# Two quarters of the combined weights made in one stay of small tiles

## The chip, the core and the metric

The kernel runs on one core of a Trainium2 chip. It is written in a language in which every instruction is given to an engine by the program: TensorE (PE in the profile) multiplies matrices, VectorE (DVE), ScalarE (ACT) and GpSimd (POOL) do the element work, SyncE (SP) issues the transfers. The engines run side by side, each takes its own instructions in order, and semaphores hold an instruction until its inputs are there and its buffer is free. The metric is the time of one execution on the device in microseconds (us); lower is better.

## The reference

Eight batches of attention with eight heads, 576 positions and 64 columns a head. Keys and values are first gathered by 32 packed queries of each head, then the full queries attend to the packed values; the result goes through a gated layer of 2048 columns, on 8 x 576 = 4608 rows.

```python
def sm_attn(qq, kk, vv):          # scale = 1/sqrt(64)
    s = scale * qq @ kk.T
    a = exp(s - max(s)); a = a / (sum(a) + 1e-09)
    return a @ vv
p_packed = sm_attn(p, k, v)              # (8, 8, 32, 64)
out = sm_attn(q, p_packed, p_packed)     # (8, 8, 576, 64)
x = out, heads side by side              # (4608, 512)
h = x @ w_in                             # w_in (512, 2048)
g = h * clip(h + 3, 0, 6) / 6
result = g @ w_out                       # w_out (2048, 512), all float32
```

## The kernel before

The second attention ends in a product with the packed values, and the layer begins with a product with w_in. Both are linear, so the kernel multiplies the packed values of a batch with w_in once: the **combined weights** M. The first product of the layer is then the attention weights a times M. M of a batch is made in four **quarters**, of 512 columns of w_in each; a quarter is two banks of PSUM. Each factor of a large product is split into a high and a low part (a_hi and a_lo, m_hi and m_lo), and three products of parts stand for one.

TensorE can be used as one tile of 128 x 128 or as several small tiles that work side by side. The products of a quarter are small (32 packed rows a head, 64 columns deep): `quarter` issues sixteen of them in tiles of 64 x 32, each with 512 columns, eight beside one another. These stretches with small tiles are called **stays** here. The other stays of a batch are the scores S of the packed queries and those of the full queries, Z (`rows_by_head`), the turned weights E and the packed values V. All else on TensorE are full-size products: the first products into ps_h (`first_product`) and the second products into acc (`product`).

PSUM has eight banks in use: four accumulators acc, two banks ps_h0 and ps_h1 (`hh`) for the first products, which take turns in them, and two banks att (`att`, ps_at in the profile) for the stays. The scores and Z put their 512 first columns into att and the 64 that are left at the end of ps_h0 and ps_h1. A quarter goes into the att banks alone. ScalarE then copies a bank to m_hi and VectorE subtracts this from the bank to m_lo, for each of the two banks.

Batch 0, and the attention of batch 1, are made in a first stage with a plan of their own. Then seven plans follow, one for each layer of batches 1 to 7; a plan also holds the attention of the batch after. In a plan each name is one step of a chain (a generator), and the order of names is the order of the instructions on every engine and queue: nothing is reordered behind it. The names: S, E, V, Z, z the attention of the next batch; m0 to m3 its quarters; lk, lq, lp, lv, lw the loads of k, q, p and the two parts of v; tk, tq the turning (transposing) of a loaded k or q on VectorE; w0 to w3 the fetches of w_in; p, s, a, b, t, g the layer's first products, gates, gate parts and second products. A name with a minus belongs to the batch of the plan before. Tables of letters say which buffer a tile takes (`HOMES`) and which of GpSimd and VectorE takes a piece of work (`ENGINES`).

Two small facts of memory matter for the change. A loaded fourth of k or q lands in one of two buffers `nat`, which the two loads of high parts of v share; `turn` transposes it into a tile `tr`, of which there are four. And w_in doesn't stay in fast memory: it is kept in a scratch copy, and each quarter is fetched anew (`fetch_w_in`, 1 MB, tile w_again), into one buffer that the low part of v uses as well.

The caller in the loop over plans, which the listing shows whole:

```python
chains = {"-" + name: chain for name, chain in chains.items()}
later_moe(chains, b)
if b + 1 < B:
    later_attention(chains, b + 1)
for name in plan.split():
    next(chains[name])
```

Of the kernel before, what the change touches and what calls it, by code (L numbers as in the profile page):

```python
# [52 lines left out]
a9 lk0 tk0 a9 a9 r5 r5 y5 lo7 y4 y4 b5 b5 li11 b5 below y5 b7 S S a10 lq0 S S b7 S S S S S x5 x5 b7 a10 h6 a11  # L53
a11 a11 h6 lo9 r6 S S a9 x5 r6 b6 x4 x5 tq0 S S S b6 b7 r6 r6 b7 h7 h7 y6 a11 m8 b7 x6 b9 x6 x6 r7 r7 m8 lq1
y7 y7 b9 x6 b9 b9 b8 m8 h8 m8 m8 li13 h8 r7 r7 x7 x7 S E x7 a13 x7 lq2 tq2 b8 b8 b8 a13 a13 a13 lo10 tq1 r8 E
r8 y6 S S y8 li12 a12 b8 lv r8 b9 h9 h9 lq3 b8 r8 b9 x8 x8 y8 b10 x8 r9 b10 b10 b10 E E r9 r9 E E li14 tq3 a12
a12 a12 h10 y9 E h10 r10 y10 r9 x9 y9 x9 r10 a14 lw1 lo12 a14 a14 x8 a14 lw0 h11 b10 b10 h11 r10 b12 b12 r10
b12 b12 V li15 V V r11 r11 a15 x9 T T a15 a15 a15 b12 x10 Z Z Z lo11 b11 b11 y10 x10 Z Z Z y11 x9 y11 b11 b11
m12 b12 m12 x10 Z m12 m12 m12 Z lo14 b14 x10 Z Z b11 r11 b11 h12 r11 h12 r12 y12 r12 y12 r12 M b14 x11 b14 b14
x11 Z Z h13 h13 r12 r13 lo13 Z r13 Z Z x12 x11 b13 b13 b13 b13 y13 y13 x11 lo15 b14 r13 r13 h14 h14 Z Z r14  # L60
b13 x12 b15 b15 r14 x12 x12 b13 b15 b15 b14 y14 h15 Z h15 x13 r14 r15 r15 b15 r14 x13 x13 x13 x14 r15 b15
stage M x14 r15 x15 x15 o0 o0 o1 o1 Z Z Z x14 x14 y15 y15 Z Z M x15 x15 M M Z Z o3 o3 o2 o2 y14
# [17 lines left out]
lk0 -a10 -b11 -b10 -b10 -b10 -o0 -b11 -p12 -p10 -t3 -a12 -p10 -Z -Z -p10 -Z -p10 -p10 -p10 -a12 -p10 -p13 -z0  # L80
-a11 -a11 -b11 -b11 -p11 -p11 -p11 -b12 -b11 -b11 -b11 -b11 -b12 -a12 -a12 -a12 -z0 -z1 -a13 -a13 -b12 -m2
-a13 -b12 -b12 -b12 -p13 -z0 -z0 -z0 lp -b12 -b12 -b12 -b12 -z1 -w1 -p11 -p11 -p11 -p11 -m2 -a13 tk0 -s18 -p12
-z0 -p12 -m2 -m2 -g18 tp -p12 -p12 -p12 -p12 -p12 -g18 -b13 -z1 -a13 lk1 -s110 -b13 -z0 -b13 -m2 -b13 -z1 -z0
-z1 -b13 -t4 -t4 -g18 -g18 -b13 -b13 -b13 -b13 -b13 -s19 -g19 -g110 -g19 -p13 -m1 -p13 -g19 -p13 -p13 -p13
-g19 -m1 -z0 lq0 -t4 -s111 -t4 -g110 -z1 -s112 -t4 -w0 -p13 -s18 -z1 -p13 -s18 -g110 -m1 -m1 -g110 -o1 -o1 -m1
# [1722 lines left out]
```

## Time and profile before

| what | value |
|---|---|
| median of three runs | 690.48 us (688.1 to 692.36) |
| the profiled execution's own time | 689.6 us |
| its span, first to last instruction | 687.8 us |
| granted clock of TensorE over the span | 0.997 of full speed |
| TensorE busy | 676.3 us, 98% of the span |
| VectorE busy | 586.5 us, 85% |
| ScalarE busy | 430.5 us, 63% |
| GpSimd busy | 313.8 us, 46% |
| moved by the DMA engines | 138.49 MB, mean 201 GB/s |

The profile is of one execution. The device time has 1.8 us around the span. The stage with batch 0 ends at about 107 us, and the last result is on its way from 684 us on; between them lies the long stretch in which the layer of one batch and the attention of the next are interleaved. Busy TensorE is busy with modelled ends of instructions that overlap in its pipeline, so the distance between starts tells what an instruction costs, and its listed duration doesn't.

### The profile page before, as it was taken

What the parts mean: (1) busy time and instruction counts of PE and PEld (TensorE: products, weight loads), DVE (VectorE), ACT (ScalarE), POOL (GpSimd) and SP (SyncE); (2) the same over time, 40 slices, a digit from 0 to 9 for tenths busy, and PEclk for the clock granted to TensorE, in tenths of its full rate; (3) what the DMA queues carried; (4) which work ended last, traced back from release to release, by engine and by line L of the source; (5) the groups of instructions that cost most, each with busy time, mean ns of one, the idle gap of its engine ahead of it and who ended that gap; (6) DMA issues with size and microseconds to landing.
All of it is one profiled execution on the core that took longest, in us unless ns stands there. A gap on an engine that the chain in (4) does not pass through costs nothing.

```text
span 687.8 us, 17158 instructions
## 1 busy us (share of the span) xinstructions
PE 676.3 (98%) x6096; PEld 599.0 (87%) x6096; DVE 586.5 (85%) x1447; ACT 430.5 (63%) x1062; POOL 313.8 (46%) x492
## 2 busy tenths in 40 slices
PE   8799999999999999999999999999999999999998
PEld 6577878787879898898989988899898989999997
DVE  3888787898998899989999879988999778978886
ACT  3899876665666466564566645665665655655553
POOL 0555544353735355553443444473534434634342
PEclk9999999999999999999999999999999999999999
DMA  9989942887899386876886786867786937434733
GB/s 259 357 206 214 233 134 80 237 208 196 218 296 211 100 280 226 194 207 219 240 228 161 178 228 219 236 146 224 175 295 146 246 116 242 158 123 131 239 118 128
DMA packets 223477, 138.49 MB, mean 201 GB/s; under 512 B 177056, under 2 KB 190880, under 8 KB 219552
## 3 DMA queue, kind: packets, MB, share of 16 engines
q1 hardware_dynamic: 223120, 137.34, 71.1%
q8 instruction: 48, 0.79, 0.5%
q14 instruction: 37, 0.30, 0.2%
q10 hardware_dynamic: 272, 0.07, 0.0%
HBM read 115.34 MB, written 22.02 MB: 200 GB/s over the span
## 4 chain that ended last, share of the span: by engine, by line
PE 91%; DMA 2%; DVE 2%; SPq 2%; ACT 2%; issue 1%; DVEq 0%; ACTq 0%
PE acc L1057 47%; PE ps_h L1079 26%; PE ps_h L770 4%; PE ps_at L1540 4%; PE acc L1237 3%; PE acc L1238 2%; PE ps_at L1438 2%; DMA raw_in<-in_moe_w_in_dram 1%; PE ps_at L1512 1%; SPq L797 1%; PE ps_at L1485 1%; DMA nat<-in_q_dram 1%; PE ps_h L1438 0%; PE ps L495 0%; SPq L516 0%
## 5 line engine op out<-in xcount | busy, mean ns | idle before, releaser
L1079 PE MATMUL ps_h<-a_hi,m_hi 128*128 128x256 f32 (+1 forms) x448 | 135.4, 302 | 0.1
L1079 PE MATMUL ps_h<-a_hi,m_lo 128*128 128x256 f32 (+1 forms) x448 | 132.5, 296 | 0.0
L1079 PE MATMUL ps_h<-a_lo,m_hi 128*128 128x256 f32 (+1 forms) x448 | 132.5, 296 | 0.0
L1057 PE MATMUL acc<-wo_hi,ge 128*128 128x256 f32 x456 | 106.9, 283 | 0.0
L1057 PE MATMUL acc<-wt,ga 128*128 128x256 f32 x684 | 104.6, 284 | 0.0
L1090 ACT ACTIVATE t<-ps_h,three 128x320 f32<-128x320 f32 (+1 forms) x126 | 63.1, 502 | 65.6 <-PE ps_h L1079 41.1
L1079 PEld LDWEIGHTS ps_h<-a_hi,m_hi 128*128 128x128 f32 x448 | 84.7, 189 | 18.1 <-DVE t L1092 5.4
L1057 PEld LDWEIGHTS acc<-wt,ga 128*128 128x128 f32 x684 | 91.3, 189 | 7.5 <-DMA wt<-t_kept 1.7
L1079 PEld LDWEIGHTS ps_h<-a_lo,m_hi 128*128 128x128 f32 x448 | 84.7, 189 | 0.9
L1079 PEld LDWEIGHTS ps_h<-a_hi,m_lo 128*128 128x128 f32 x448 | 84.7, 189 | 0.0
L1057 PEld LDWEIGHTS acc<-wo_hi,ge 128*128 128x128 f32 x456 | 80.9, 189 | 3.9 <-ACT e L1453 0.8
L1101 POOL TENSOR_TENSOR ga<-t,ga 128x256 fp32r<-128x256 f32 (+1 forms) x72 | 56.7, 787 | 45.7 <-ACT ga L1099 39.2
L1101 POOL TENSOR_TENSOR ge<-t,ge 128x256 fp32r<-128x256 f32 x68 | 51.8, 761 | 46.6 <-ACT ge L1099 35.2
L1101 POOL TENSOR_TENSOR gf<-tb,gf 128x256 fp32r<-128x256 f32 x57 | 44.1, 773 | 62.3 <-ACT gf L1099 56.4
L1090 ACT ACTIVATE tb<-ps_h,three 128x256 f32<-128x256 f32 (+1 forms) x98 | 49.1, 501 | 35.5 <-PE ps_h L1079 27.2
L1092 DVE SCALAR_TENSOR_TENSOR t<-t,ps_h 128x320 f32<-128x320 f32 (+1 forms) x126 | 56.2, 446 | 16.8 <-ACT t L1090 15.7
L1099 ACT CAST ga<-t 128x256 fp32r<-128x256 f32 (+1 forms) x114 | 47.9, 420 | 25.6 <-PE acc L1057 11.0
L1057 PE MATMUL acc<-wo_lo,ge 128*128 128x256 f32 x228 | 63.9, 280 | 0.0
L1057 PE MATMUL acc<-wo_hi,gf 128*128 128x256 f32 x228 | 59.0, 285 | 0.0
L1057 PE MATMUL acc<-wo_hi,ga 128*128 128x256 f32 x228 | 58.8, 282 | 0.0
L1092 DVE SCALAR_TENSOR_TENSOR tb<-tb,ps_h 128x256 f32<-128x256 f32 (+1 forms) x98 | 43.6, 445 | 13.3 <-ACT tb L1090 12.7
L1099 ACT CAST ge<-t 128x256 fp32r<-128x256 f32 x98 | 39.5, 405 | 23.8 <-DVE t L1257 18.5
(265 smaller groups left out, 1846.5 us busy)
## 6 DMA issues: line engine op xcount, KB each, us to landing
wt<-t_kept SPq DMA_DIRECT2D x162, 256.0 KB, 4.1
w_again<-w_kept SPq DMA_DIRECT2D x24, 1024.0 KB, 5.3
out_dram<-osb SPq DMA_DIRECT2D x34, 256.0 KB, 2.5
nat<-in_k_dram SPq DMA_DIRECT2D x112, 72.0 KB, 4.7
nat<-in_q_dram SPq DMA_DIRECT2D x112, 72.0 KB, 2.9
raw_in<-in_moe_w_in_dram SPq DMA_DIRECT2D x10, 512.0 KB, 5.7
raw_out<-in_moe_w_out_dram SPq DMA_DIRECT2D x10, 512.0 KB, 4.4
t_kept<-wt SPq DMA_DIRECT2D x6, 768.0 KB, 5.2
```

Source lines behind the costliest of these rows:

```text
L770: nc.tensor.matmul(h[:, hf, :HS], mm[:, g, fs], aa[:, hf * HS:(hf + 1) * HS], start=(g == 0 and i == 0), stop=(g == NG - 1 and i == 2),)
L797: nc.sync.dma_start(out=t.rearrange("p h c d -> p h (c d)"), in_=src[0].rearrange("(a x) r d -> x a r d", x=2)[g, h0:h0 + n, :C0 * P].rear ...
L1057: nc.tensor.matmul(out, lhs[x], rhs[y], start=first and i == 0, stop=last and i == 2, skip_group_check=True)
L1079: nc.tensor.matmul(h, mm[:, g, fs], aa[:, t0:t0 + n], start=(g == 0 and i == 0), stop=(g == NG - 1 and i == 2),)
L1090: nc.scalar.activation(out=t[:, :n], in_=h, func=AF.Relu, bias=three)
L1092: nc.vector.scalar_tensor_tensor(out=t[:, :n], in0=t[:, :n], scalar=6.0, in1=h, op0=ALU.min, op1=ALU.mult)
L1099: nc.scalar.copy(out=hi, in_=x)
L1101: on(name, engine).tensor_sub(out=lo, in0=x, in1=hi.bitcast(F32))
L1237: nc.tensor.matmul(bank(x), hi, both(i, r), start=fresh, stop=False, skip_group_check=True)
L1238: nc.tensor.matmul(part, lo, block(i, r)[0], start=False, stop=stop, skip_group_check=True)
L1438: nc.tensor.matmul(to[x][NPK * a:NPK * a + NPK], lhs[at, a], rhs[a][at].rearrange("p t i -> p (t i)")[:, cols], start=True, stop=True,)
L1540: nc.tensor.matmul(t[x][NPK * a:NPK * a + NPK], pps[b % 2][at, a], w_in_sb[n][at, :, a], start=True, stop=True)
```

## The change

Of batches 2 to 7, two quarters are made in one stay. The function `quarters` takes one or two numbers of quarters: the first goes into the att banks as before, the second into ps_h0 and ps_h1, whole. The second one's sixteen products stand first, then the first one's; the copies and subtractions come in the same order. The three quarters that remain for batch 1 are made singly. Batches 2 to 7 have chains m only for the second of each two, and each makes two quarters.

Both w_in quarters of a stay have to be there at once. The first is fetched into the buffer w_again as before. The second is fetched into a tile with the tag tr (w_tr): the four tiles tr of a fourth each become one tile for all four, in one buffer, which the turned k, the turned q and the fetched quarter now use one after another.

```diff
     def turn(which, b, a):
-        t = ap.tile([P, T, 32], F32, name="tr", tag="tr", bufs=4)
+        if ("tr", which, b) not in state:
+            state["tr", which, b] = ap.tile([P, NPAIR, T, 32], F32, name="tr", tag="tr", bufs=1)
+        t = state[which, b, a] = state["tr", which, b][:, a]
         nc.vector.transpose(out=t, in_=state.pop(("nat", which, b, a)))
-        state[which, b, a] = t
...
-    def quarter(b, n):
-
-        t = [att(x) for x in range(2)]
-        for a in range(NPAIR - 1, -1, -1):
...
+    def quarters(b, *ns):
+
+        banks = [[att(x) for x in range(2)], hh][:len(ns)]
+        for n, t in reversed(list(zip(ns, banks))):
+            for a in range(NPAIR - 1, -1, -1):
+                for x in (1, 0):
+                    at = slice(64 * x, 64 * x + 64)
+                    nc.tensor.matmul(
+                        t[x][NPK * a:NPK * a + NPK], pps[b % 2][at, a], w_in_sb[n][at, :, a], start=True, stop=True
+                    )
+        yield
+        for n, t in reversed(list(zip(ns, banks))):
+            hi, lo = m_tiles(b, n)
+            for x in range(2):
+                nc.scalar.copy(out=hi[:, x], in_=t[x])
+                yield
+                nc.vector.tensor_sub(out=lo[:, x], in0=t[x], in1=hi[:, x].bitcast(F32))
+                yield
+
+    def fetch_w_in(n, second):
+        if second:
+            t = ap.tile([P, NPAIR, T, 32], F32, name="w_tr", tag="tr", bufs=1)
+            t = t.rearrange("p a t i -> p (a t i)")[:, :FPC * DM]
+        else:
+            t = wr.tile([P, FPC * DM], F32, name="w_again", tag="w_in0")
+        w_in_sb[n] = t.rearrange("p (f a e) -> p f a e", f=FPC, a=NPAIR)
+        nc.sync.dma_start(out=t, in_=w_kept[n])
         yield
...
-        for n in range(NCH):
-            chains[f"w{n}"] = fetch_w_in(n)
-            chains[f"m{n}"] = quarter(b, n)
+        made = made_in(b)
+        for k, n in enumerate(made):
+            chains[f"w{n}"] = fetch_w_in(n, k % 2)
+            if k % 2:
+                chains[f"m{n}"] = quarters(b, made[k - 1], n)
...
-        chains = {f"m{n}": quarter(1, n) for n in range(1, NCH)}
+        chains = {f"m{n}": quarters(1, n) for n in range(1, NCH)}
```

The plans of the layers and the two tables are written anew; of them the diff shows rows of names alone, as in the first lines of the plan of batch 1:

```diff
-lk0 s00 s01 g00 g01 g00 g00 g00 g00 kw kw -m1 s02 -m1 g01 g01 kw s03 s00 t0 -m1 -m1 -m1 -m2 g03 g03 g01 g01
+s00 g00 s01 lk0 g00 g00 -m1 g01 g01 g00 g00 g01 g01 g01 s02 -m1 -m1 -m1 -m1 s00 kw kw g02 s03 g03 s00 -m2 g02
```

What moves on the engines is seen in their rows. The first place is TensorE in the plan of batch 2, where the last quarter of batch 2 was made before. ps_at are the att banks and ps_h those of the first products (the numbers tell tiles apart), acc is an accumulator, g a gate, pps the packed values.

```order
L1540 MATMUL ps_at_2767<-w_again,pps 32x512
L1540 MATMUL ps_at_2766<-w_again,pps 32x512
L1540 MATMUL ps_at_2767<-w_again,pps 32x512
L1540 MATMUL ps_at_2766<-w_again,pps 32x512
L1540 MATMUL ps_at_2767<-w_again,pps 32x512
L1540 MATMUL ps_at_2766<-w_again,pps 32x512
L1079 MATMUL ps_h_1570<-a_hi,m_hi 128x256
L1079 MATMUL ps_h_1570<-a_lo,m_hi 128x256
L1079 MATMUL ps_h_1570<-a_hi,m_lo 128x256
```

Before, a first product into ps_h follows a quarter at once. The same engine with the change, from the end of the second pair's first half on:

```order
L1542 MATMUL ps_h_1564<-w_tr,pps 32x512
L1542 MATMUL ps_at_2733<-w_again,pps 32x512
L1542 MATMUL ps_at_2732<-w_again,pps 32x512
L1542 MATMUL ps_at_2733<-w_again,pps 32x512
L1542 MATMUL ps_at_2732<-w_again,pps 32x512
L1542 MATMUL ps_at_2733<-w_again,pps 32x512
L1542 MATMUL ps_at_2732<-w_again,pps 32x512
L1542 MATMUL ps_at_2733<-w_again,pps 32x512
L1542 MATMUL ps_at_2732<-w_again,pps 32x512
L1058 MATMUL acc<-wo_hi,g_2688 128x512
L1058 MATMUL acc<-wo_lo,g_2688 128x512
L1058 MATMUL acc<-wo_hi,g_2688 128x512
```

The quarter from w_tr stands in the ps_h banks, the one from w_again in the att banks behind it. Three second products of 512 columns stand between the stay and the next first product into ps_h.

The second place is VectorE in the plan of batch 3, where quarters of batch 3 are split and k of batch 4 is turned. tr<-nat is the turning, m_lo the subtraction, t and tb gates that read a first product, osb a result on its way out. Before:

```order
L760 STREAM_TRANSPOSE tr<-nat 128x576
L1548 TENSOR_TENSOR m_lo<-ps_at_3913,m_hi 128x512
L1101 TENSOR_TENSOR ge<-t,ge 128x256
L1092 SCALAR_TENSOR_TENSOR t<-t,ps_h_1570 128x320
L1257 TENSOR_TENSOR t<-t 128x128
L1092 SCALAR_TENSOR_TENSOR tb<-tb,ps_h_1571 128x320
L760 STREAM_TRANSPOSE tr<-nat 128x576
L1312 SCALAR_TENSOR_TENSOR osb<-acc,osb 128x256 x3
```

The turns stand one at a time, and m_lo reads ps_at alone. With the change:

```order
L762 STREAM_TRANSPOSE tr<-nat 128x576 x2
L1551 TENSOR_TENSOR m_lo<-ps_h_1564,m_hi 128x512
L1551 TENSOR_TENSOR m_lo<-ps_h_1565,m_hi 128x512
L1551 TENSOR_TENSOR m_lo<-ps_at_4077,m_hi 128x512
L1551 TENSOR_TENSOR m_lo<-ps_at_4078,m_hi 128x512
L1258 TENSOR_TENSOR t<-t 128x128
L1271 TENSOR_TENSOR t<-t,tb 128x2x128
L1277 TENSOR_TENSOR tb<-tb,t 128x128
L1102 TENSOR_TENSOR gf<-tb,gf 128x256
L1093 SCALAR_TENSOR_TENSOR t<-t,ps_h_1564 128x320
L762 STREAM_TRANSPOSE tr<-nat 128x576 x2
L1093 SCALAR_TENSOR_TENSOR tb<-tb,ps_h_1565 128x320
```

The four subtractions of a pair follow one another, those of the ps_h banks first. The two gates that read ps_h_1564 and ps_h_1565 come behind them. Two turns of the next k stand behind the last m_lo, and more behind these: k can't be turned into tr before the quarter in it has been used.

On SyncE's queue the 24 fetches stay 24, twelve into w_again and twelve into w_tr, and the loads of k, q, p and v stand in other places between them. VectorE has 1455 rows in place of 1442 in the order, and GpSimd 482 in place of 489: some gate subtractions have changed engines.

## Rows read from the trace of the kernel before

**Rows 1.** The chain that ended last; busy us (x count) by engine, 107:684.

```profile
PE 91%; DMA 2%; DVE 2%; SPq 2%; ACT 2%; issue 1%; DVEq 0%; ACTq 0%
...
107.00:684.00 577.00, 576.47 (x5202) 520.51 (x5201) 504.38 (x1277) 346.89 (x905) 263.01 (x441) 1.00 0.70 197
```

**Rows 2.** Waits of TensorE: total us, times, longest.

```profile
PE ps_h L770 <- ACT m_hi L506: 2.1, 1, 2.1
...
PE ps_at L1512 <- DMA v_high<-in_v_dram: 0.2, 1, 0.2
```

**Rows 3.** Timeline of TensorE (start us, us) around a quarter; 170.83: second wave.

```profile
170.05 0.28 PE L1057 MATMUL acc<-wo_lo,ge 128*128 128x256 f32 x1
170.17 0.28 PE L1057 MATMUL acc<-wo_hi,ge 128*128 128x256 f32 x1
...
170.38 1.09 PE L1540 MATMUL ps_at<-w_again,pps 64*32 64x512 f32 x16
...
170.83 0.64 PE L1540 MATMUL ps_at<-w_again,pps 64*32 64x512 f32 x8
...
171.40 0.39 PE L1079 MATMUL ps_h<-a_hi,m_hi 128*128 128x256 f32 x1
171.62 0.28 PE L1079 MATMUL ps_h<-a_lo,m_hi 128*128 128x256 f32 x1
```

**Rows 4.** Timeline of TensorE, the scores' stay; 140.46: second wave.

```profile
140.03 1.06 PE L1438 MATMUL ps_at<-tr,p_tr 64*32 64x512 f32 x16
...
140.46 0.64 PE L1438 MATMUL ps_at<-tr,p_tr 64*32 64x512 f32 x8
...
141.03 0.50 PE L1057 MATMUL acc<-wo_hi,g 128*128 128x512 f32 x1
```

**Rows 5.** Timeline of TensorE and ScalarE, one quarter and its first copy.

```profile
178.78 0.66 PE L1540 MATMUL ps_at<-w_again,pps 64*32 64x512 f32 x8
...
180.00 0.59 ACT L1546 CAST m_hi<-ps_at 128x512 fp32r<-128x512 f32 x1
```

**Rows 6.** Groups by line: busy us, mean ns | idle before them, releaser.

```profile
L1546 ACT CAST m_hi<-ps_at 128x512 fp32r<-128x512 f32 x54 | 30.9, 586 | 7.3 <-PE ps_at L1540 7.1
...
L760 DVE STREAM_TRANSPOSE tr<-nat 128x576 f32<-128x576 f32 x56 | 43.0, 770 | 3.1 <-DMA nat<-in_q_dram 3.1
...
L1548 DVE TENSOR_TENSOR m_lo<-ps_at,m_hi 128x512 fp32r<-128x512 f32 x54 | 36.1, 679 | 2.2 <-ACT m_hi L1546 2.0
```

**Rows 7.** SyncE's issues, one load of k; last its fourth's landing.

```profile
494.07 2.14 SPq L516 DMA_DIRECT2D nat<-in_k_dram  x4
...
495.53 0.68 SPq L516 DMA_DIRECT2D nat<-in_k_dram  x1
...
nat<-in_k_dram SPq DMA_DIRECT2D x1, 72.0 KB, 2.5
```

**Rows 8.** The same of a load issued straight behind a fetched quarter.

```profile
346.53 4.12 SPq L516 DMA_DIRECT2D nat<-in_k_dram  x4
...
349.63 1.01 SPq L516 DMA_DIRECT2D nat<-in_k_dram  x1
...
nat<-in_k_dram SPq DMA_DIRECT2D x1, 72.0 KB, 6.0
```

**Rows 9.** DMA issues: count, KB each, median us to landing.

```profile
w_again<-w_kept SPq DMA_DIRECT2D x24, 1024.0 KB, 5.3
...
nat<-in_k_dram SPq DMA_DIRECT2D x112, 72.0 KB, 4.7
```

**Rows 10.** Timeline of TensorE, the stays of packed values of batches 2 and 3.

```profile
159.68 0.32 PE L1512 MATMUL ps_at<-v_nat,et 128*32 128x64 f32 x8
...
162.29 0.39 PE L1079 MATMUL ps_h<-a_hi,m_hi 128*128 128x256 f32 x1
...
226.25 0.32 PE L1512 MATMUL ps_at<-v_nat,et 128*32 128x64 f32 x8
...
227.56 0.38 PE L1057 MATMUL acc<-wt,ga 128*128 128x256 f32 x1
```

More of the change, by code (lines that the diff above doesn't have):

```diff
@@ L52 @@
 r3 lo5 y1 a8 b3 b6 b6 b6 x3 r4 tp a8 r4 a8 x3 a10 x3 b5 h5 h5 x3 r4 tk1 r4 x4 x4 x4 y3 y3 b5 b5 r5 r5 li9 a8
[L53 to L62, printed above, removed]
+a9 lk0 tk0 a9 a9 r5 r5 y5 lo7 y4 b5 b5 li11 below y5 y4 S b5 S a10 lq0 S S b7 b7 S S S S S b7 x5 x5 a11 a10 h6
+h6 a11 a11 lo9 r6 S S a9 x5 r6 b6 x4 x5 tq0 S b7 b7 S S b6 r6 r6 h7 h7 y6 a11 m8 b9 x6 x6 x6 r7 m8 lq1 tq1 y7
+r7 y7 b9 x6 b7 b9 b9 b8 m8 h8 m8 m8 h8 li13 r7 r7 x7 x7 S E x7 b8 b8 b8 a13 x7 lq2 tq2 a13 a13 y6 lo10 r8 E r8
+S S a13 y8 li12 a12 b8 r8 b9 h9 h9 lq3 b8 r8 b9 x8 x8 y8 b10 r9 b10 b10 b10 x8 E E r9 r9 lv E E li14 tq3 b10
+a12 a12 a12 h10 r9 y9 h10 E r10 y10 y9 x9 x9 r10 a14 lw1 lo12 a14 a14 x8 a14 r10 lw0 h11 b10 h11 b12 b12 r10
+b12 b12 V V V r11 r11 li15 a15 x9 T T a15 a15 a15 b12 x10 Z Z Z lo11 b11 b11 y10 x10 Z Z Z y11 x9 b11 b11 m12
+b12 m12 x10 Z m12 m12 m12 Z lo14 b14 Z x10 Z Z b11 r11 b11 h12 r11 h12 r12 y12 M y11 lo13 r12 b14 b14 r12 b13
+x11 x11 b13 b13 b14 h13 r12 h13 r13 y13 b13 r13 y13 x11 Z b14 x11 r13 b14 y12 b13 x12 h14 h14 x12 x12 r13 r14
+Z x12 Z r14 lo15 b15 Z Z Z b15 b15 h15 h15 r14 b13 x13 r15 r15 y15 Z Z x13 x13 x13 y14 b15 r14 x14 b15 x14 b15
+stage r15 r15 M y14 M M x15 x15 o0 o0 Z o1 Z o1 Z y15 x14 x15 Z Z M x14 x15 o3 o3 Z o2 o2
 """
@@ L80 @@
[L80 to L84, printed above, removed]
@@ new lines @@
+w2 a13 z0 b12 t0 b12 b12 p11 a13 a13 p11 p11 p10 b12 p11 b12 b12 z0 p13 a13 z0 p12 b13 b12 z1 z1 s18 p11 b12
+b12 b13 g18 b13 b13 a13 p12 p12 p12 p12 p12 p12 s19 z1 g18 b13 b13 b13 z0 b13 z1 z0 g18 g18 g19 b13 z1 g19 z0
+s110 p13 g110 z1 g110 z0 g110 p13 p13 g110 t5 o1 p13 z1 b13 z0 m1 o1 m1 g19 m1 p13 p13 p13 s18 m1 m1 m1 m1 m1
+g19
+    """,
+    """
+lp tp -t4 -t4 -z1 -t4 -s111 -g111 -s18 -z1 -t5 -t5 -g111 -t5 -z0 -t5 -s112 -g111 -s19 -s113 -g111 -s19 lk1 -t3
+-g112 -g112 -t5 -t5 -g112 -t3 -ek -g113 -w0 -g112 -t5 lk0 -s114 -g114 -o1 -s110 -s110 -s111 -s112 -o1 -t4
@@ L1532, in second_scores @@
                 yield
-    def quarter(b, n):
-        t = [att(x) for x in range(2)]
-        for a in range(NPAIR - 1, -1, -1):
-            for x in (1, 0):
-                at = slice(64 * x, 64 * x + 64)
-                nc.tensor.matmul(
-                    t[x][NPK * a:NPK * a + NPK], pps[b % 2][at, a], w_in_sb[n][at, :, a], start=True, stop=True
-                )
-        yield
-        hi, lo = m_tiles(b, n)
-        for x in range(2):
-            nc.scalar.copy(out=hi[:, x], in_=t[x])
-            yield
-            nc.vector.tensor_sub(out=lo[:, x], in0=t[x], in1=hi[:, x].bitcast(F32))
-            yield
-    def fetch_w_in(n):
-        t = w_in_sb[n] = wr.tile([P, FPC, NPAIR, P], F32, name="w_again", tag="w_in0")
-        nc.sync.dma_start(out=t.rearrange("p f a e -> p (f a e)"), in_=w_kept[n])
+    def quarters(b, *ns):
[7 more added lines that the diff above has]
+                    )
+        yield
+        for n, t in reversed(list(zip(ns, banks))):
[13 more added lines that the diff above has]
+        nc.sync.dma_start(out=t, in_=w_kept[n])
         yield
```

315 lines of the change are left out of this document (155 added, 160 removed), and 124 rows, old and new, of the table ENGINES.

## The prediction

> **What bounds the kernel now.** I read the chain that ended last and the busy time by stretches first [rows 1]: the chain is 91% TensorE, and between 107 and 684 us TensorE is busy 576.47 of 577.00 us. VectorE is the next engine with 504.38, 87%. The waits of TensorE come second [rows 2]: the longest entries are 2.1 us and less, each happened once, and only one, 0.2 us on v_high, names something later than the first products of the first batch. So in the long middle stage nothing can get shorter by making another engine faster. Time is won there only by giving TensorE less to do, and the reader should look for work that is not streaming columns.
>
> Such work is seen in the third view, the timeline around one quarter of the combined weights [rows 3]. Full-size products of 256 columns start every 0.12 us. The last one before the quarter starts at 170.17, the first small one at 170.38 (0.21 later, so 0.09 is lost); the second wave of eight starts at 170.83; the next full-size product starts at 171.40, and its successor at 171.62 (0.22, so 0.10 is lost on the way out). In all, 171.62 - 170.17 - 2 x 0.12 = 1.21 us for one quarter.
>
> How much of that belongs to the stay and how much to the columns? The scores' stay [rows 4] has the same small tiles and more of them: sixteen products of 64 columns come first, and then two waves of 512 columns, which start at 140.03 and 140.46, 0.43 apart; the next full-size product starts at 141.03. So in a stay that is already open a wave of 512 columns costs about 0.43 us, two of them (a quarter) 0.86, and a quarter in a stay of its own costs 1.21. The fixed part of a stay is 0.35 us.
>
> **The change part by part.**
>
> *Twelve stays fewer.* Batches 2 to 7 have four quarters each, 24 in all, and each pair becomes one stay; the three quarters of batch 1 stay single. The number of products is the same, 5202 instructions in the order on either side. Gain: 12 x 0.35 = 4.2 us on the engine that sets the end. The other end of this term comes from the entry, exit and rest taken apart: 0.09 + 0.10, and the 1.02 us between [rows 3] less two waves, 2 x 0.43 = 0.86, leave 0.16; again 0.35. If waves in a four-wave stay were as far apart as the first two in rows 3 (0.45), it would be 12 x 0.31 = 3.7. I take 4.2.
>
> *Both halves' banks are held.* The second quarter of a pair is written into ps_h0 and ps_h1 over their whole 512 columns. So the pair waits until ScalarE and VectorE have read the last first product from there, and the next first product waits until the quarter has been split into m_hi and m_lo. Queued behind a waiting first product are all products of the older pairs, since TensorE works in order. The pieces [rows 5, 6]: after a stay that starts at 178.78 the copy to m_hi starts at 180.00, 1.22 later; it takes 0.59 and the subtraction to m_lo 0.68. In the new stay the quarter in ps_h comes first, so its copy can start 1.22 after the stay's start, ps_h0 is free at about 1.22 + 0.59 + 0.68 = 2.49, plus a tenth for two semaphores, and ps_h1 a further 0.68 later, 3.27. The stay's last wave gives way at 1.02 + 0.86 = 1.88. The order puts other products there: the shortest cover before the first product is 0.70 us (two stays; the other ten have 1.0 us or more), which ends at 2.58. That fits with nothing to spare, if ScalarE and VectorE take the quarter at once. In one of the twelve, three subtractions of a gate stand between the two of m_lo, and ps_h1 comes some 0.35 us late there. Bounds: nothing, or one subtraction, 0.68, at each of the twelve, 8.2 us. The cover is there in the order, so I take 0.05 each, 0.6 us.
>
> *The turned k wait for the second pair.* Before, tr is four small tiles, and k of the next batch can be turned at any time after q's scores. Now one tile holds all of k, or q, or a fetched quarter, so the four turns of k stand between the batch's second pair and the scores S. Only two nat buffers exist, so two of the four loads can't be issued before the first two turns. This happens five times, for batches 3 to 7. Worked out for the boundary that is shown on VectorE: tr is free when its quarter is done, 1.1 after the stay's start; two turns of 0.77 [rows 6] end at 2.65; the third load's four issues begin at 1.9 and the fourth's at about 4.0, as four issues take 2.14 [rows 7]; a load that meets a quiet queue is there 495.53 + 2.5 - 494.07 = 4.0 us after its first issue [rows 7], at 8.0; the last turn ends at 8.8. TensorE reaches the scores 1.88 + 7.6 = 9.5 after the stay's start (the order's products there, at 0.12 us for 256 columns [rows 3] and in proportion for 320 and 512). The other four boundaries have 10.4 to 12.2 us, and later second turns. All five hold as long as a load takes less than about 4.7 to 6.2 us, 5.3 in the mean. A load behind a fetched quarter took 349.63 + 6.0 - 346.53 = 9.1 [rows 8]. In the new order no quarter is fetched between the pair and S, only parts of 256 KB and rows of the result stand just ahead. Bounds: 0 and 5 x (9.1 - 5.3) = 19 us; nearest is the quiet load, and I take 0.3 each, 1.5 us.
>
> *Fetches.* They stay 24 of 1 MB. Two are issued close together now, 12 us and more ahead of their use by the order, against a median of 5.3 us to landing [rows 9]. I cost them at nothing; the cover is those 12 us, and if a pair took 8 us longer than that, a stay would be late by as much.
>
> *The queues' new order.* The loads of v are issued elsewhere. One stay of packed values took 162.29 - 159.68 = 2.61 us for want of v_high, where the next took 227.56 - 226.25 = 1.31 [rows 10]. Bounds: 1.3 us back, or as much lost in another batch. I take half of the gain, 0.7. About twenty subtractions of gates go from GpSimd to VectorE; even at m_lo's 0.68, which is twice as wide, they are 14 us on an engine with 577 - 504 = 73 us to spare; they cost nothing unless they stand ahead of a bank's release, which is in the second term.
>
> Sum against the profiled execution's 689.6 (span 687.8, 1.8 us around it): 689.6 - 4.2 + 0.6 + 1.5 - 0.7 = 686.8. The median of the three runs, 690.48, lies 0.9 above the profiled one and the lowest, 688.1, lies 1.5 below, so I don't shift it.
>
> **The rivals.**
>
> *The banks eat the gain.* Each pair needs four bank-wide subtractions of 0.68, 2.7 us of VectorE, for 1.88 us of TensorE, and two of the four hold the banks that every first product needs. If each of the twelve releases is late by 0.35 us, as the one worked out above, 4.2 us go back: 689.6 - 4.2 + 4.2 = 689.6; the change then does not do what it says. For it: VectorE is at 87%. Against: of the two-wave stays the trace has 24 and TensorE waits at none of them [rows 2]. The Trainium skill has a rule that speaks for this rival, TensorEngine Tiling (Array Packing), Performance Considerations: small tiles speed up TensorE but not the emptying of PSUM, whose copy may then become the bottleneck. By that rule the time would be this 689.6; the 0.68 of m_lo against 0.43 a wave agrees with it, the empty list of waits does not.
>
> *Late k, slower than before.* It decides at a load of 5.3 us. At 7 us the five boundaries are late by 0.8, 2.3, 2.0, 2.1 and 1.4 us, 8.6 in all: 689.6 - 4.2 + 0.6 + 8.6 - 0.7 = 693.9. For it: the median of the k loads' pieces to landing is 4.7 us each [rows 9], and pieces follow one another. Against: the slow ones had 1 MB just ahead of them. The Trainium skill says in DMA: Bandwidth & Descriptors, Queues, rings and completion order, that on each of the 16 engines descriptors of a queue are taken in ring order; by that a load pays for whatever was issued just ahead, which is what rows 7 and 8 show.
>
> *Everything holds.* No new wait and no v_high wait: 689.6 - 4.2 - 1.3 = 684.1.
>
> **How the numbers follow.** Forecast 686.8 with 0.60 (684.8 to 688.7 by itself), the banks 0.15, late k 0.13, everything holds 0.12. The range goes from 683.3 to 692.5: it takes in the third rival and the near half of the late loads. One per cent, about what a measurement of this kernel can tell from no change, is 6.9 us: 683.6 and 697.4. Only the third rival can pass the lower bound, from a start as low as the fastest run's 688.1, 0.09; late k with loads of 8 us passes the upper one, 0.07; the rest, 0.84, lies between.
>
> **What would show it.** In the changed kernel's trace: twelve stays with thirty-two small products and 1.86 to 1.90 us from the first to the next full-size product; the first product after them 0.12 us behind its predecessor, not more; the scores of batches 3 to 7 without a gap before them, and their last turn of k ended ahead; k loads of about 4 us behind the second pair. I would be wrong if stays of four waves cost more than 2.1 us in all, if gaps stand before first products after a pair, or if the span is filled with waits for nat.

## The result, and the profile after

The changed kernel takes 693.91 us in the median of 20 runs (688.9 to 696.43), the kernel before 689.14 us (20 runs, 687.32 to 692.36) beside it. The ratio is 1.0054, with a 95% interval of 1.0037 to 1.0071: it is slower, by 3.7 us of about 690 (the two medians lie 4.8 apart). The forecast was 686.8 with a range to 692.5. The profiled execution took 694.26 us, with a span of 692.2, 4.4 us more than before.

The chain that ended last and the busy time by stretches, of the changed kernel (they answer to [rows 1]):

```profile
PE 82%; DVE 6%; DMA 6%; SPq 3%; ACT 2%; issue 1%; DVEq 0%; ACTq 0%
...
107.00:687.00 580.00, 575.44 (x5205) 524.00 (x5204) 510.60 (x1291) 350.33 (x910) 254.90 (x427) 1.00 0.68 196
```

The chain was 91% TensorE and is 82%. In the middle stage TensorE is idle 580.00 - 575.44 = 4.6 us, where it was 0.5. So the stage no longer has one bound from end to end. The waits of TensorE from 105 us on (us in total, times, longest) answer to [rows 2]; before, v_high was the only one of this stretch:

```profile
PE acc L1058 <- DVE ge L1102: 1.9, 1, 1.9
PE ps_at L1486 <- ACT e L1467: 1.2, 1, 1.2
PE acc L1058 <- DMA wt<-t_kept: 0.6, 1, 0.6
PE acc L1238 <- DVE osb L1338: 0.4, 1, 0.4
PE ps_at L1513 <- DMA v_high<-in_v_dram: 0.3, 1, 0.3
PE ps_h L1439 <- DVE tb L1093: 0.2, 1, 0.2
```

No first product waits for an m_lo. The merged stay itself is as it was forecast. TensorE's timeline around the first pair of batch 2 (it answers to [rows 3]):

```profile
179.86 1.09 PE L1542 MATMUL ps_h<-w_tr,pps 64*32 64x512 f32 x16
180.74 1.06 PE L1542 MATMUL ps_at<-w_again,pps 64*32 64x512 f32 x16
181.73 0.38 PE L1058 MATMUL acc<-wo_hi,gf 128*128 128x256 f32 x1
181.96 0.28 PE L1058 MATMUL acc<-wo_lo,gf 128*128 128x256 f32 x1
```

From the first small product to the next full-size one it is 1.87 us. With the same 0.21 ahead of it and 181.96 - 181.73 = 0.23 behind, less two pitches of 0.12, the pair costs 2.07 us, where two single quarters cost 2 x 1.21 = 2.42. That is 0.35 us a pair; the twelve pairs cost 2.07 to 2.16.

What has come in its place stands on VectorE. The waits of its turns for loads from 100 us on were these in the kernel before (first fence) and are these in the changed one (second):

```profile
DVE tr L760 <- DMA nat<-in_q_dram: 2.7, 2, 1.8
```

```profile
DVE tr L762 <- DMA nat<-in_q_dram: 6.7, 5, 3.0
DVE tr L762 <- DMA nat<-in_k_dram: 1.4, 2, 0.9
```

The worst place is batch 4. SyncE's issues there, of the changed kernel (start us, us in which they were issued):

```profile
286.08 4.41 SPq L516 DMA_DIRECT2D nat<-in_k_dram  x8
290.58 2.09 SPq L632 DMA_DIRECT2D v_nat<-in_v_dram  x4
292.72 1.27 SPq L623 DMA_DIRECT2D v_nat<-in_v_dram  x2
294.09 5.18 SPq L516 DMA_DIRECT2D nat<-in_q_dram  x8
299.36 2.96 SPq L1208 DMA_DIRECT2D wt<-t_kept  x6
302.42 2.33 SPq L516 DMA_DIRECT2D nat<-in_q_dram  x4
```

The second pair's stay starts at 284, and only after the first turns behind it do the last two loads of k go out, from 286.08 on. All four of q come behind these. In the kernel before, the first load of q for this batch (one load is four issues) went out 7.4 us ahead of the scores S (first two rows below); now it goes out with them (third row, against 294.09 above):

```profile
278.45 1.94 SPq L516 DMA_DIRECT2D nat<-in_q_dram  x4
285.85 0.34 PE L1438 MATMUL ps_h<-tr,p_tr 64*32 64x64 f32 x16
...
294.03 0.35 PE L1439 MATMUL ps_h<-tr,p_tr 64*32 64x64 f32 x16 [0.23 <-DVE tb L1093]
```

In batches 3 to 7 this lead of q was 6.1 to 27.5 us before; with the change the first load goes out between 4.1 us ahead of S and 0.1 behind it. The third load of q is issued at 302.42, behind six transfers of wt. VectorE and TensorE meet it here (the bracket is the idle time ahead and what ended it; VectorE's rows first, then TensorE's):

```profile
306.23 0.42 DVE L1102 TENSOR_TENSOR ga<-t,ga 128x256 fp32r<-128x256 f32 x1
309.61 0.78 DVE L762 STREAM_TRANSPOSE tr<-nat 128x576 f32<-128x576 f32 x1 [2.96 <-DMA nat<-in_q_dram]
310.31 0.38 DVE L1102 TENSOR_TENSOR ge<-t,ge 128x256 fp32r<-128x256 f32 x1
...
308.61 0.28 PE L1058 MATMUL acc<-wo_lo,ge 128*128 128x256 f32 x1
310.75 0.50 PE L1058 MATMUL acc<-wo_hi,ge 128*128 128x256 f32 x2 [1.86 <-DVE ge L1102]
```

The turn stands in front of a gate in VectorE's order. It waits 2.96 us for q; the gate ge behind it needs nothing of q, but TensorE needs ge, and waits 1.86 us. The stretches after it (busy us by engine, then the granted clock of TensorE) show a second price:

```profile
308.00:310.00 2.00, 0.89 (x8) 0.68 (x6) 0.39 (x1) 0.00 (x0) 0.00 (x0) 1.00 1.05 145
310.00:312.00 2.00, 1.25 (x9) 1.21 (x10) 1.09 (x3) 0.41 (x1) 0.24 (x1) 1.00 0.87 228
312.00:314.00 2.00, 2.00 (x13) 2.00 (x11) 1.60 (x4) 0.46 (x2) 0.00 (x0) 0.56 1.02 285
314.00:316.00 2.00, 2.00 (x12) 2.00 (x12) 1.97 (x7) 0.46 (x2) 0.91 (x1) 0.59 0.63 140
316.00:318.00 2.00, 1.84 (x53) 1.54 (x52) 1.49 (x5) 1.40 (x4) 1.31 (x2) 1.00 0.33 90
```

After the wait TensorE is busy all of 312 to 316, and yet only 21 products start in these 4 us (the 25 of the two rows count those that lie across an edge too): the clock was granted at 0.56 and 0.59, close to the lower of its two levels (1.2 and 2.4 GHz). Products of 256 columns then start 0.21 us apart and not 0.12, which costs some 1.5 us on top of the wait. It doesn't follow each time: in the run e1_old_stage1, told of below, TensorE waits nearly as long, and is granted the full clock all through (its wait, and the two stretches behind it):

```profile
329.78 0.39 PE L968 MATMUL acc<-wo_hi,ga 128*128 128x256 f32 x1 [1.78 <-DVE ga L1012]
330.00:332.00 2.00, 2.00 (x17) 1.96 (x17) 1.97 (x9) 0.49 (x2) 0.00 (x0) 1.00 0.85 227
332.00:334.00 2.00, 2.00 (x18) 1.96 (x17) 2.00 (x7) 1.72 (x5) 0.00 (x0) 1.00 1.02 375
```

From the starts of all of TensorE's products in the two traces, each against its pitch, the sum is: quarters -4.2; packed values -0.4; single waits of over 0.15 us +4.6; shorter gaps, the half clock among them, +2.1; and 2.3 us by which the first single quarter comes later (the product ahead of it starts at 119.16, where it was 116.87). Together that is 4.4, the difference of the spans. Which gap counts as which is a matter of some 0.3 us.

### The profile page after: what moved, and what is told of

Its sections match the earlier page's. It is cut to its first block, busy times and chain, and to the rows that moved or that the text cites. A ratio compares the mean times of both kernels' runs of the same rounds, so it can differ in the third digit from the quotient of the medians.

```text
span 692.2 us, 17152 instructions
## 1 busy us (share of the span) xinstructions
PE 673.8 (97%) x6096; PEld 600.4 (87%) x6096; DVE 592.8 (86%) x1459; ACT 431.7 (62%) x1062; POOL 306.5 (44%) x480
## 4 chain that ended last, share of the span: by engine, by line
PE 82%; DVE 6%; DMA 6%; SPq 3%; ACT 2%; issue 1%; DVEq 0%; ACTq 0%
PE acc L1058 42%; PE ps_h L1080 24%; PE acc L1238 3%; PE ps_h L771 3%; PE ps_at L1542 2%; PE ps_h L1542 2%; PE acc L1239 1%; DMA nat<-in_q_dram 1%; PE ps_at L1439 1%; DMA room<-in_q_dram 1%; SPq L516 1%; PE ps_at L1513 1%; DVE tr L762 1%; DMA raw_in<-in_moe_w_in_dram 1%; DMA wt<-t_kept 1%
## 5 line engine op out<-in xcount | busy, mean ns | idle before, releaser
L1080 PE MATMUL ps_h<-a_hi,m_hi 128*128 128x320 f32 (+1 forms) x448 | 135.5, 302 | 0.0
L1080 PE MATMUL ps_h<-a_hi,m_lo 128*128 128x320 f32 (+1 forms) x448 | 132.8, 296 | 0.0
L1080 PE MATMUL ps_h<-a_lo,m_hi 128*128 128x320 f32 (+1 forms) x448 | 132.8, 296 | 0.0
L1058 PE MATMUL acc<-wt,ga 128*128 128x256 f32 x684 | 106.8, 285 | 0.6 <-DMA wt<-t_kept 0.6
L1102 POOL TENSOR_TENSOR ge<-t,ge 128x256 fp32r<-128x256 f32 x63 | 49.7, 789 | 44.7 <-ACT ge L1100 24.8
L1102 POOL TENSOR_TENSOR ga<-t,ga 128x256 fp32r<-128x256 f32 (+1 forms) x64 | 52.6, 821 | 35.6 <-ACT ga L1100 29.1
L1102 POOL TENSOR_TENSOR gf<-tb,gf 128x256 fp32r<-128x256 f32 x48 | 38.2, 795 | 64.5 <-ACT gf L1100 47.7
L1100 ACT CAST gf<-tb 128x256 fp32r<-128x256 f32 x98 | 39.6, 404 | 24.5 <-DVE tb L1093 19.2
```

What stands on the lines that cost most here:

```text
L1058: nc.tensor.matmul(out, lhs[x], rhs[y], start=first and i == 0, stop=last and i == 2, skip_group_check=True)
L1080: nc.tensor.matmul(h, mm[:, g, fs], aa[:, t0:t0 + n], start=(g == 0 and i == 0), stop=(g == NG - 1 and i == 2),)
L1100: nc.scalar.copy(out=hi, in_=x)
L1102: on(name, engine).tensor_sub(out=lo, in0=x, in1=hi.bitcast(F32))
```

## The experiments

The ratio is always to the kernel before, run beside it on the same chip (its medians were 689.1 to 690.35); 0.001 is 0.7 us.

| run | median us | ratio, 95% interval |
|---|---|---|
| the changed kernel | 693.91 | 1.0054 (1.0037 to 1.0071) |
| e3_light | 685.45 | 0.9932 (0.9910 to 0.9955) |
| e4_before_light | 688.57 | 0.9984 (0.9967 to 1.0001) |
| e7_light_q | 686.55 | 0.9963 (0.9942 to 0.9984) |
| e8_light_k | 688.37 | 0.9988 (0.9965 to 1.0012) |
| e9_light_split | 689.51 | 1.0008 (0.9987 to 1.0028) |
| e10_split | 696.51 | 1.0104 (1.0083 to 1.0125) |
| e2_split | 693.55 | 1.0054 (1.0027 to 1.0080) |
| e1_old_stage1 | 693.14 | 1.0037 (1.0017 to 1.0056) |
| e5_load_order | 696.09 | 1.0072 (1.0049 to 1.0095) |
| e11_alias | 692.59 | 1.0055 (1.0033 to 1.0077) |
| e12_nat3 | 691.49 | 1.0034 (1.0014 to 1.0054) |
| e14_own_early | 731.25 | 1.0623 (1.0603 to 1.0642) |
| e15_own_spread | 746.38 | 1.0804 (1.0766 to 1.0842) |
| e19_own_soon | 700.63 | 1.0151 (1.0114 to 1.0188) |
| e20_before_late | 719.26 | 1.0415 (1.0384 to 1.0447) |
| e16_act_queue | 801.65 | 1.1616 (1.1581 to 1.1652) |
| e17_pool_queue | 797.29 | 1.1551 (1.1517 to 1.1585) |
| e18_before_act | 778.05 | 1.1264 (1.1227 to 1.1300) |

**Is it the loads?** Four runs make the loads of k and q light: one transfer with rows of 2.3 KB for each, in place of four with pieces of 128 bytes. The same bytes land in another arrangement, so these kernels attend with shuffled k, shuffled q or both.

```diff
         t = ap.tile([P, T, 32], F32, name="nat", tag="nat", bufs=2)
+        if b > 1:
+            nc.sync.dma_start(
+                out=t.rearrange("p t i -> p (t i)"),
+                in_=src[b, 2 * a:2 * a + 2].rearrange("h r d -> (h r d)").rearrange("(p x) -> p x", p=P),
+            )
+            return t
         for h in range(2):
```

For one of the two the condition is `b > 1 and src is q` (or `k`).

> The changed kernel with each load of a fourth of k or q, from batch 2 on, made by one transfer of 128 rows of 2.3 KB in place of four with pieces of 128 bytes: the same bytes land, but in another arrangement, so the attention of batches 2 to 7 is that of shuffled k and q. Theory B (the loads are what VectorE waits for): all waits of the turns go, at all boundaries, 693.9 - 4 to 5 = 689 to 690. Rival C (the loads are not the cause): 693.9 within 1 us.

> The kernel before with the same light loads of k and q as in the run e3_light (one transfer with rows of 2.3 KB for each fourth, from batch 2 on, so that its attention is that of shuffled k and q). Theory B (the kernel before had room for its loads, and only the change made them late): it loses only its own small waits, 0.2 to 1.5 us: 688 to 689.7 beside 689.9. Rival D (light loads help any kernel, since they take less of the queues and DMA engines): it falls by about as much as the changed kernel did, 6 to 8 us, to 682 to 684.

> The changed kernel with light loads of q alone (batches 2 to 7 attend with shuffled q); the loads of k stay as they are. VectorE's turns waited 6.7 us for q and 1.4 us for k in the changed kernel's trace. If the late q holds the gates up (theory B): most of the 8.4 us that light loads of both gave come back, 687. If k is the one that sets the boundary and q only comes after it: 691 to 692.

> The changed kernel with light loads of k alone (batches 2 to 7 attend to shuffled k). If q holds the gates up by itself: 691 to 693, and VectorE's turns still wait 5 us or more for q. If the late k pushes q back, as both go through two buffers: 687 to 689, and the waits for q fall to under 3 us.

The changed kernel falls from 1.0054 to 0.9932, by 0.0122 or 8.4 us. The kernel before falls by 0.0016, 1.1 us, and its interval holds 1. So light loads are no gift to any kernel (rival D falls); about 7.3 us of late loads came with the change (by the four intervals together, nearly 3 us more or less), and once they are gone the changed kernel is 0.0052 or 3.6 us faster than its control. Light loads also have a quarter of the issues: from 150 us on SyncE spends 17 us on issuing k and q, and 107 in the changed kernel. So the 7.3 us are the price of these loads whole, of issuing and landing together. Light q alone brings 0.0091 (6.3 us), light k alone 0.0066 (4.6 us), together not 10.9 but 8.4: they lie in one chain. With light k and q as it was, the turns still wait for q, but less than the 6.7 us above:

```profile
DVE tr L768 <- DMA nat<-in_q_dram: 4.0, 4, 1.3
```

So k pushes q back, though not below the 3 us that the expectation named, and q also waits by itself. Rival C (VectorE has too much to do) falls: with light loads VectorE does the same work, and TensorE waits 0.9 us in all from 105 us on:

```profile
PE acc L1064 <- DMA wt<-t_kept: 0.5, 1, 0.5
PE acc L1244 <- DVE osb L1344: 0.4, 1, 0.4
```

**Is the merging worth what it was priced at?** Two runs take the twelve pairs apart: a chain n issues the first quarter's products (m those of the second alone), and its step stands behind the next step of second products.

```diff
-                chains[f"m{n}"] = quarters(b, made[k - 1], n)
+                chains[f"m{n}"] = quarters(b, made[k - 1], n)
+                chains[f"n{n}"] = first_quarter(b, made[k - 1])
...
--m0 tk3 p04 p04
+-m0 tk3 p04 -n0 p04
```

> The changed kernel with light loads of both, and with every pair of quarters in two stays: the first quarter's sixteen products stand behind the next step of second products, and all 24 quarters are single stays. Beside e3_light (685.45) it prices the merging where no load is waited for. Theory (a merged stay is worth 0.35 us and TensorE is the bound): 685.45 + 4.2 = 689.7. Rival (the time is waited out elsewhere): 685 to 687.

> The changed kernel with all twelve pairs in two stays (in the run e2_split the second stay of six pairs had come straight behind the first, so that only six were apart). Loads are as in the changed kernel. With light loads the same edit cost 4.1 us. Theory (the price of a stay holds here too): 693.9 + 4.1 = 698. Rival (the loads set the pace at the boundaries, and a longer stay is only a shorter wait): 693.9 to 695.5, as half of the edit, in e2_split, cost nothing that could be measured.

With light loads the split costs 0.0076, 5.2 us (4.06 by the medians); with the loads as they are 0.0050, 3.5 us (2.6 by the medians); each with an interval of about 2 either way. Both agree with 4.2 and neither with nothing. An earlier form split only six of the pairs:

> The changed kernel with the two quarters of each of the twelve pairs in stays of their own: one step of second products (three or four full-size products) is put between them, all else is in place. Theory (the merged stay is worth what the trace shows, 2 x 1.215 - 2.077 = 0.35 us each, and nothing hides it): 693.9 + 12 x 0.35 = 698.1. Rival (TensorE has waits behind the pairs anyway, so the saved time is only waited out): 694 to 695.

It gave 1.0054, no difference from the changed kernel; half of the price, 2.1 us, is about what the two intervals together leave open, so I had been too quick to read the rival out of it.

**Does the first stage cost 2.3 us?** The changed kernel with the plan, the t buffers and the engine choices of the first stage of before:

```diff
...
-    "t": ("0100100110101010...
+    "t": ("0100101001010101...
```

> The changed kernel with the first stage of the kernel before: its plan, its buffers of t and its choice of engines for batch 0 and the attention of batch 1; the layers of batches 1 to 7 stay as changed. In the two traces the first single quarter starts 2.3 us later in the changed kernel (116.87 and 119.16 us after the span's start), and most of that is one wait of TensorE for z from VectorE, 1.4 us, and one for v_high, 0.5 us. Theory A (the new order of the first stage costs these 2.3 us): 693.9 - 2.3 = 691.6. Rival (one execution's chance, the rest is in the layers): 693.9 as the changed kernel, and the first single quarter starts within 0.5 us of 119.2 again.

The ratio falls by 0.0017, 1.2 us, and the intervals overlap. In the traces of runs that share the changed first stage the product ahead of the first single quarter starts anywhere from 115.85 (e12_nat3) to 120.91 us (e15_own_spread), so the 2.3 us of one pair of traces can be chance alone. What is left of it isn't told from nothing.

**Can the loads be put right by order?** Three loads are moved in the plan of batch 3:

```diff
-S p06 a07 ... lv ... lq0 ... lq2 S S ... tq0 f01 ... tq2 ... lq3 tq3 l0 ... lq1 tq1 V
+S p06 a07 ... lq0 ... lq2 lv S S ... tq0 lq3 f01 ... tq2 lq1 ... tq3 l0 ... tq1 V
```

> The changed kernel with three loads moved on SyncE's queue in the plan of batch 3, and nothing else: the low part of v goes behind the second load of q, the third load of q ahead of six loads of wt, the fourth ahead of a transfer of e_again. Theory B (the load of q for batch 4 lands late, its turn stops VectorE for 2.96 us, TensorE waits 1.9 us for a gate behind it, and then runs some 3 us at half clock): the turns find q landed, 2.0 + 1.6 us come back and part of the 0.6 us at the packed values, 693.9 - 4 = 690. Rival C (the gates are late because VectorE has too much to do there, whatever q does): 693.9 within 1 us, and TensorE's wait for ge stays over 1 us.

Theory B's 690 didn't come. The time is 1.0072, not less than the changed kernel's 1.0054, and yet it isn't rival C either, which let TensorE go on waiting for ge: it waits for wt instead, which had stood ahead of the load:

```profile
309.13 0.80 PE L1070 MATMUL acc<-wt,gf 128*128 128x512 f32 x1 [3.98 <-DMA wt<-t_kept]
```

**What makes them late?** First a control and a third buffer; two m_lo are laid over their m_hi, since the fast memory is full otherwise:

```diff
-            )
+            ) if j not in (2, 3) else (mp[1].tile([P, NG, NB], F32R, name="m_hi", tag=f"m_hi{j}"),) * 2
...
-        t = ap.tile([P, T, 32], F32, name="nat", tag="nat", bufs=2)
+        t = ap.tile([P, T, 32], F32, name="nat", tag="nat", bufs=3)
```

> A control for the next two: the changed kernel with two of the four m_lo buffers laid over their m_hi (the first products of these quarters then use the low part twice), which frees 8 KB a partition. All instructions are the same. It should take 693.9 within 1.5 us; if it differs, the next two are compared with this one.

> The control e11_alias with a third buffer nat for the loads of k, q and the high part of v; the order on all queues is the same. If the two buffers keep the loads late (the third and fourth of k wait for turns, q for these): the turns' waits fall from 8 us to under 3 us, and the time to 688 to 690. If SyncE's order and the transfers themselves keep them late: 692 to 694.

The control is the changed kernel again (1.0055). The third buffer gives 1.0034, 1.4 us less with overlapping intervals, and the turns still wait 5.7 us for q and 1.0 for k: two buffers alone aren't the cause. Then the fetched quarter gets a buffer of its own, and the turns of k are moved up, in three ways:

```diff
-            t = ap.tile([P, NPAIR, T, 32], F32, name="w_tr", tag="tr", bufs=1)
-            t = t.rearrange("p a t i -> p (a t i)")[:, :FPC * DM]
+            t = mp[1].tile([P, FPC * DM], F32, name="w_tr", tag="w_own")
...
-(batch 3) -w0 ... -m0 tk3 ... tk0 ... lk2 ... tk2 lk1 tk1 ... S ... lq0 ... lq2
+(e19)     -w0 tk3 lk2 ... tk0 lk1 ... -m0 ... tk2 lq0 ... tk1 lq2 ... S
```

> The control e11_alias with the second fetched quarter in a buffer of its own (w_tr doesn't share tr), and in the plans of batches 2 to 6 the turns of the next k some 24 steps earlier, two of them ahead of the second pair, with the loads of k behind them and two loads of q following. If the sharing of tr, which puts the turned k behind the second pair, is the root: 688 to 690, with the turns' waits under 3 us. If moved loads only move the waits, as in e5_load_order: 692 to 697.

> The run e14_own_early mended: there the loads of k that were moved up stood ahead of fetched quarters on SyncE's queue, and these came 7.5 us late. Now, with w_tr in its own buffer and the two m_lo laid over m_hi as in e11_alias, the first turns stand up to 100 steps ahead of the second pair (as far as the loads of k allow), each followed at once by its next load, and the third and fourth turn 70 steps later, each followed by a load of q; the fetches go ahead of loads that would wait. If the sharing of tr is the root: 687 to 690 beside 692.6 of e11_alias, and turns wait under 3 us for k and q together. If the loads stay late because SyncE's queue and the two nat buffers are full in any order: 692 or more.

> As e15_own_spread (w_tr in a buffer of its own, two m_lo laid over m_hi), but the turns moved up by less: in the plans of batches 2 to 6 the first two turns of k and the loads behind them stand straight after the last fetch of a quarter, so that no fetch stands behind them; the last two turns some 45 to 60 steps later, each with a load of q. If the sharing of tr, by which k's turns come behind the second pair, is the root: 687 to 690 beside 692.6 of e11_alias, with turns waiting under 3 us. If two nat buffers and one queue keep loads late in any such order: 692 to 697.

All three are misses. In the first two, loads that wait for a nat buffer stopped SyncE's queue, and fetched quarters behind them came late (by up to 7.5 and 10.0 us, each a wait of TensorE). In e19 no fetch of the batch stands behind, and the turns' waits do fall, from 8.7 in the control to 4.6 us; but wt is late now. Waits of VectorE's turns, then of TensorE, in e19:

```profile
DVE tr L594 <- DMA nat<-in_q_dram: 2.8, 3, 1.5
DVE tr L594 <- DMA nat<-in_k_dram: 1.8, 1, 1.8
...
PE acc L1070 <- DMA wt<-t_kept: 4.2, 1, 4.2
```

The other direction, the places of the changed kernel put into the kernel before (batch 3 as an example; of the plan only the names that move, and some around them, are shown):

```diff
-lk3 lk0 tk0 -m3 lk1 tk1 -w0 lk2 tk3 lq0 -m0 tk2 S lv lq3
+lk0 -m3 lk1 -w0 tk0 tk1 -m0 lk3 tk3 lk2 tk2 lq0 S lv lq3
```

> The kernel before, single stays and all, with k's four turns, the last two loads of k and the first two of q put as many steps from the scores S as they have in the changed kernel, in the plans of batches 2 to 6 (a load goes behind the batch's last fetch of a quarter, and a load of q stays 25 steps ahead of its turn). It computes the same as before. If these places alone make the loads late: 689.5 + 5 to 8 = 694.5 to 697.5, and the turns wait 6 us or more for k and q (2.7 us in the kernel before). If something else of the changed kernel does: 689 to 691.

It is 29 us slower, far more than the 5 to 8 of the expectation, and VectorE's turns wait:

```profile
DVE tr L588 <- DMA nat<-in_q_dram: 17.2, 7, 8.3
DVE tr L588 <- DMA nat<-in_k_dram: 7.9, 5, 2.2
```

With nothing merged and no shared tile, late places of the turns, and of the loads that go with them, are enough to make k and q late. Why that costs so much more here than in the changed kernel isn't shown; that this order wasn't laid for it is a guess.

**Another queue?** The loads are issued by another engine:

```diff
-                nc.sync.dma_start(
+                (nc.sync if b < 2 else nc.scalar).dma_start(
```

(`nc.gpsimd` in e17_pool_queue.)

> The changed kernel with the loads of k and q of batches 2 to 7 issued by ScalarE and not by SyncE; buffers and the order of names are the same. SyncE's other transfers (wt, v, quarters) then don't stand behind a load that waits for a nat buffer, nor the loads behind them; but ScalarE waits for the nat buffer itself. If the order on the one queue is what makes loads late: 688 to 690. If ScalarE's gates and copies pay for it: above 694.

> The changed kernel with the loads of k and q of batches 2 to 7 issued by GpSimd, which is 44% busy. If the order on SyncE's queue is what makes loads late, and GpSimd can issue them without cost: 687 to 690. If its gate subtractions are held up by the issues or by the wait for a nat buffer: above 694.

> The kernel before with its loads of k and q of batches 2 to 7 issued by ScalarE: the control of e16_act_queue. Its loads had room, so it should gain nothing: 689 to 691, or lose what ScalarE's issues cost; that loss is then also in e16_act_queue.

All three lose 88 to 112 us, the control too. The transfers themselves land no later: in e16 2.8 us (k) and 2.6 us (q) after their issue, against 3.3 and 3.2 in the changed kernel. They are issued too late. In e16 the turns wait:

```profile
DVE tr L762 <- DMA nat<-in_q_dram: 32.0, 12, 4.8
DVE tr L762 <- DMA nat<-in_k_dram: 22.4, 6, 8.6
```

SyncE computes nothing and runs ahead of the others to the next transfer whose buffer is free; ScalarE and GpSimd come to a load only when their work ahead of it in the order is done. That this lead is the cause is my reading of these rows; no run varied the lead alone. A rival stands beside it, the issuing itself: on ScalarE it takes 0.51 us a piece (median of 192 pieces, 104 us in all), on GpSimd 0.667 (127 us), and the engine's own work stands behind it. Here in e16 a gate (tb) stands behind the four issues of one load of q:

```profile
238.61 4.28 ACTq L516 DMA_DIRECT2D nat<-in_q_dram  x4
243.02 0.47 ACT L1091 ACTIVATE tb<-ps_h,three 128x256 f32<-128x256 f32 x1 [4.35 <-DMA nat<-in_q_dram]
```

TensorE waits 23 us for ScalarE's gates g, ga and gf in that run, and, from 105 us on, for none of them in the changed kernel. The runs don't tell how much of the loss is lead and how much is issuing. The Trainium skill says in Perfetto Trace Analysis, DMA Optimizations, that balancing transfers across the engines that can issue them may help where the generation of descriptors is the bottleneck. No run here shows whether it is; moving these loads cost 88 to 112 us.

No run that computes what the reference does is faster than the kernel before.

## Why the prediction was wrong

*Twelve stays fewer, 4.2 us:* right. The trace shows 0.35 us for each, the two splits 5.2 and 3.5 us for all by their ratios.

*Both halves' banks, 0.6 us:* the cover held, and the cost was next to nothing. No first product waits for an m_lo; eleven pairs cost 2.07 to 2.10 us, one 2.16.

*Fetches, nothing:* right. w_tr and w_again land 6.8 and 6.3 us after their issue (median), and TensorE waits for none.

*The queues' new order, -0.7 us:* -0.4 in the six stays of packed values together. v_high is late by less, in other places. Thirteen gates went from GpSimd to VectorE, not some twenty.

*The turned k wait for the second pair, 1.5 us:* this is the term that failed. Late loads cost 7.3 us by the two pairs of light runs, k and q together. The loads of q have no term in the prediction: they were put at nothing without a reason. I followed k to the scores S and stopped there: "all five hold as long as a load takes less than about 4.7 to 6.2 us". As to S that was right: the loads of k behind the pair took 3.7 to 5.3 us from first issue to last landing, and S itself waited 0.2 us in one place, for a gate. What I didn't follow is what is queued behind k. The four loads of q go through the same two nat buffers, so they go out only as the turns of k free these, and q lost its lead ahead of S. The turns of q stand on VectorE in front of gates that have nothing to do with q, so VectorE is held, and then TensorE: the wait of 1.86 us and, in this execution, a stretch at half clock behind it. Light q alone brings back 6.3 us of the 8.4, light k alone 4.6: k pushes q back, and q is what is mostly waited for.

*The rivals.* "Late k, slower than before" gave 693.9 and had 0.13. The number is what was measured; its mechanism (k late at S when a load takes 7 us) isn't: the loads of k were faster than that, and the price came one step later, through q. That the number fits is luck. "The banks eat the gain" didn't happen. "Everything holds" gave 684.1, and e3_light, where no load is waited for, measured 685.45.

What stays open is whether the shared tile tr is the root, or the places that the new plans give to loads and turns. e20 shows that late places are enough to make k and q late; e19 that earlier turns make the turns wait less. But no order that I tried turned this into time, since SyncE's one queue then made wt or a quarter late. Whether an order exists that keeps the 4 us isn't shown.

## What to carry to other kernels

When a step is moved behind another, follow not only the one who waits for it but everything that goes through the same buffers and queues after it, up to the next point of slack; here most of the price came two steps on, at q and not at k. An in-order engine that waits for a transfer holds every instruction behind it: ask for each moved load what stands behind its consumer on that consumer's engine. And make the load light (same bytes, easy pattern) in both kernels before arguing about order: one pair of runs split a loss of 4 us into a gain of 4 and a price of 7.

## What the runs showed that I had not expected

A wait of 1.86 us on a TensorE that had been busy was followed, after 1.5 us more of work, by 3.3 us at half clock (granted 0.56 and 0.59 in the two rows), so that it cost nearly twice its length; waits of 1.78 us (e1_old_stage1) and 2.37 us (e14_own_early) were followed by no fall of the granted clock, one of 1.94 us (e20_before_late) was. Moving the same loads from SyncE to ScalarE or GpSimd cost 88 to 112 us, though their pieces landed about as fast (medians of 2.5 to 3.5 us, where the two kernels have 2.9 to 4.7). And the changed kernel's runs spread more (688.9 to 696.43) than those of the kernel before (687.32 to 692.36), as one would expect of a kernel whose end hangs on when transfers land and not on TensorE alone; this last is argued, not tested.
